# Keys of four chunks turned by transfers and VectorE instead of TensorE, and the bonus sums of two chunks taken from a natural layout, in a linear-attention plus cosine-FFN kernel

## Chip, cores and metric

One core of a Trainium2 chip runs the whole kernel. The metric is device time in microseconds (us) from start to end, the median of several executions. The profile is one execution; its span is what the engines' own records cover.

## What is computed

Inputs `r, k, v, w` are 4 batches x 8 heads x 768 steps x 48 values in float32, `u` is 8 x 48. The attention keeps a 48 x 48 state per batch and head; its output goes through a feed-forward layer with the gate h*cos(h), 384 to 2048 to 384.

```python
def _attn_ref(r, k, v, w, u):
    state = np.zeros((B, H, D, D), dtype=np.float32)
    for t in range(S):
        kt, vt, rt, wt = (k[:, :, t], v[:, :, t], r[:, :, t], w[:, :, t])
        cur = np.einsum('bhd,bhe->bhde', u[None] * kt, vt)
        y[:, :, t] = np.einsum('bhd,bhde->bhe', rt, state + cur)
        state = wt[:, :, :, None] * state + np.einsum('bhd,bhe->bhde', kt, vt)

def _moe_ref(x, w_in, w_out):
    h = x @ w_in
    return ((h * np.cos(h)) @ w_out)
```

The term `cur` gives, for each step and head, v times the number sum(r*u*k). The text calls that number the bonus sum.

## The kernel before

The 768 steps of each batch are cut into 6 chunks of 128, so there are 24 chunks; they are taken in the order "first chunk of all four batches, second chunk of all four, ...". Chunks 0 to 3 are therefore the first ones of their batches, chunks 4 to 7 the second ones. Two neighbouring chunks make a block (12 blocks, `BLK`), and each block goes through 8 FFN units of two 128-wide slices (96 units, numbered t).

In the chunk's own layout, `tt`, the heads' 48 values lie on partitions (two heads at rows 0 and 64, four pairs along the free axis) and time runs along the free axis. For each chunk j the steps have short names, which the tables of order use:

- `e`, `f`: the two scans of the decays on VectorE (L283, L289; f begins with a reciprocal, L288); `k`, `r`: keys and queries multiplied by them (L298 whole for chunks 0 to 5; L300 and L302, half each, from chunk 6 on); `W`: a small copy of the chunk's whole decay.
- Bonus sums. Chunks 0 to 5 (`BY_PE = 6`): `q` multiplies r and k on VectorE (L272), `pc` takes the sums over u by four TensorE products (L311), `cd` copies them out on ScalarE. From chunk 6 on: a natural copy of r and k (time on partitions) is loaded into the tile `rk` (L262, 384 KB, SP's queue), `m` and `u` multiply by k and by u (L320, L321), `c` reduces (L325). `A` places the sums on the diagonal of the score tiles `asb` (L335, POOL).
- `a`: scores k times r on TensorE (`pa`, L374 or L382); `P`: their lower triangle is copied into `asb` (L393 or L396, VectorE).
- Turned keys, time on partitions, which the state's update needs. Chunks 0 to 7 (`BY_BLOCKS = 8`): `t` is four TensorE transposes into `pt` (L408), `K` copies them to `kn` (L171; ScalarE in the opening, VectorE later). From chunk 8 on: `t` is 16 small transfers on SP's queue from `tt` to a tile of blocks (L425; 16 or 8 KB each), `K` one VectorE transpose of 32 x 32 blocks (L429).
- `s`, per block: products of v and `kn` into `pst` (L444), the first chunk's half before the second's; `n` adds them to the states (L454). `o` (L479, L485) and `p` (L507, L513) make the block's attention output, `xh` and `xl` turn it into the high and low part `xT` for the FFN.
- FFN unit: `mm1` (L594), then `I` (ScalarE, L557), `S` (VectorE, L560), `N` (ScalarE, L573), `M` (VectorE, L574), `H` (high part, mostly ScalarE, L171) and `L` (low part, POOL, L174, two halves), then `mm2` (L612), two units behind `mm1`.

The opening, units 0 to 15, is one table of tokens, `START`: TensorE, VectorE, ScalarE, POOL and SP execute their instructions in the order of these tokens. In it the FFN weights are loaded and split too (`raw`, `wg`, `wl`, `wy`, `wc`, `wx`). Units 16 to 23 follow the eight rows of `FIRST`, later units those of `PLAN`; there the four compute engines follow the rows' order, while the scheduler places SP's transfers. A row is one unit; "K+3" in block 2 means step K of chunk 7.

The tile kinds that matter: `tt` has 5 buffers, `rkt` 2, `kn` 2, `asb` 4. The two tiles `tops` serve the weights' conversion in the opening and the blocks of turned keys afterwards, by the parity of the chunk. SP's queue issues in order: an instruction that waits holds all behind it.

Of the kernel before, what the change touches and what calls it, by code (L numbers as in the profile page):

```python
# [66 lines left out]
ld0 e0 f0 ld1 raw2 raw1 q0 e1 k0 D14 pc0 r0 q1 cd0 v0 v1 raw0 f1 D10 a0 W0 wg2 wl2 A0 k1 pc1 wl1 r1 wy2 P0 cd1 D6 a1 wc2  # L67
t0 wg1 A1 ld3 ld2 wg0 W1 t1 P1 v5 wx2 wy1 o0 K0 K1 xh0.0 xp0.0 s0 wl0 e3 q3 wc1 xa0.0 wy0 wc0 xh0.1 wp1 f3 pc3 xp0.1
wv1 wx0 xa0.1 q2 e2 n0 k3 f2 raw3 k2 m0.0 m1.0 pc2 t3 r3 I0 r2 wg3 raw4 v2 wl3 cd2 v3 raw5 wy3 m0.1 cd3 S0 t2 a3 A3 K3
K2 A2 P3 ld7 wl4 wg4 a2 ld5 wc3 wg5 N0 raw8 raw6 P2 s1 wx3 raw9 n1 q5 o1 xh1.0 xl1.0 raw7 m1.1 xh1.1 pc5 xl1.1 M0 m0.2  # L70
wl5 Wa3 I1 wy4 m1.2 S1 m0.3 H0 cd5 wc4 N1 wy5 wc5 wg6 I2 m1.3 M1 wx4 wl6 I3 Hv1 L0 mm2.0 m0.4 wx5 S2 N2 wy6 S3 wg9 wl9
M2 m1.4 N3 L1 mm2.1 H2 I4 e5 wc6 wy9 L2 m0.5 M3 m1.5 S4 H3 wx6 N4 wg7 raw14 v4 L3 ld4 M4 raw11 m0.6 mm2.2 wl7 wcv9 wy7
wx9 mm2.3 wg8 I5 S5 wc7 wx7 H4 N5 M5 k5 m1.6 m0.7 t5 raw10 W2 wl8 wg11 I6 m1.7 H5 wy8 L4 mm2.4 S6 wc8 L5 I7 q4 N6 S7 N7
wl11 wx8 M6 mm2.5 H6 M7 H7 m0.8 m1.8 A5 wl10 L6 I8 wg10 f5 wy11 K5 m0.9 L7 S8 e4 ld6 raw13 raw12 m1.9 N8 M8 I9 wc11
wy10 wg12 wc10 mm2.6 mm2.7 raw15 d4 S9 N9 H8 r5 wx11 a5 wx10 M9 wl12 wl13 H9 L8 L9 m0.10 wy12 wc12 m1.10 wg13 m0.11 I10
k4 P5 wx12 S10 m1.11 N10 mm2.8 I11 pc4 t4 wy13 M10 wg15 wl15 Wa5 wc13 W4 d5 S11 cd4 f4 wx13 N11 K4 M11 m0.12 r4 H10 A4
# [917 lines left out]
```

## Time and profile before

| what | us |
|---|---|
| median of 3 runs | 499.8 (499.64 to 502.58) |
| the profiled execution | 499.0 |
| its span | 497.3 |
| TensorE busy | 489.9 (99%) |
| VectorE busy | 388.3 (78%) |
| ScalarE busy | 258.1 (52%) |
| POOL busy | 204.4 (41%) |

"Busy" for TensorE counts overlapping matmuls once. The span is 1.7 us shorter than its execution's time, and that execution 0.8 us shorter than the median. The TensorE clock was granted in full through nearly the whole span. Times in a timeline count from the span's start; a timeline's row merges neighbours of one kind, and "x" is their count.

### The profile page before, as it was taken

How to read it: one execution, taken by the hardware profiler on the slowest of the kernel's cores; microseconds unless marked ns; L12 is line 12 of the kernel's file. 1: busy time of each engine (PE TensorE's matmuls, PEld its weight loads, DVE VectorE, ACT ScalarE, POOL GpSimd, SP SyncE). 2: the span in 40 equal slices, each digit the busy share in tenths (PEclk: the TensorE clock that was granted, in tenths of full speed). 3: DMA queues.
4: the chain of work that ended last, by engine and by line, in shares of the span. 5: the costliest groups of instructions: out<-in, count | busy, mean ns of one | idle time of the engine just before them, and what ended most of it. 6: DMA issues, size and time to landing. Idle time of an engine off the chain costs nothing.

```text
span 497.3 us, 13512 instructions
## 1 busy us (share of the span) xinstructions
PE 489.9 (99%) x5592; PEld 475.3 (96%) x5592; DVE 388.3 (78%) x682; ACT 258.1 (52%) x447; POOL 204.4 (41%) x274
## 2 busy tenths in 40 slices
...
GB/s 276 414 404 130 380 153 1 131 100 97 38 92 195 19 200 78 17 200 32 58 175 42 80 154 60 80 94 121 75 44 156 65 8 121 33 65 128 33 2 35
DMA packets 38832, 57.01 MB, mean 115 GB/s; under 512 B 23536, under 2 KB 30192, under 8 KB 38768
## 3 DMA queue, kind: packets, MB, share of 16 engines
...
q8 instruction: 45, 0.74, 0.6%
...
q10 hardware_dynamic: 144, 0.10, 0.1%
...
## 4 chain that ended last, share of the span: by engine, by line
PE 80%; DVE 11%; ACT 3%; DMA 2%; issue 2%; SPq 1%; POOL 1%; DVEq 0%; ACTq 0%
PE ph L594 35%; PE acc L612 34%; PE pa L382 2%; PE py L479 2%; DVE rr L560 2%; PE py L485 2%; DVE rr L574 2%; DMA raw<-wts 1%; PE py L513 1%; DVE tt L289 1%; DVE asb L396 1%; DVE ee L283 1%; PE pst L444 1%; ACT rr L557 1%; PE py L507 1%
## 5 line engine op out<-in xcount | busy, mean ns | idle before, releaser
L174 POOL TENSOR_TENSOR gs<-rr,gs 128x256 fp32r<-128x256 f32 x188 | 155.5, 848 | 225.9 <-ACT gs L171 213.2
L594 PE MATMUL ph<-xT,w 128*128 128x256 f32 x1728 | 219.6, 281 | 0.2 <-ACT xT L531 0.2
L594 PEld LDWEIGHTS ph<-xT,w 128*128 128x128 f32 x1728 | 212.3, 188 | 3.6 <-PE py L513 1.6
L612 PE MATMUL acc<-w,gs 128*128 128x384 f32 x1152 | 215.4, 337 | 0.0
L612 PEld LDWEIGHTS acc<-w,gs 128*128 128x128 f32 x1152 | 196.2, 188 | 0.5 <-issue 0.2
L573 ACT ACTIVATE rr<-rr,quarter 128x512 f32<-128x512 f32 x96 | 69.5, 724 | 90.8 <-DVE rr L560 90.8
L560 DVE SCALAR_TENSOR_TENSOR rr<-rr,ph 128x512 f32<-128x512 int32 x96 | 65.6, 684 | 54.2 <-ACT rr L557 51.2
L171 ACT CAST gs<-rr 128x512 fp32r<-128x512 f32 x91 | 56.5, 621 | 70.6 <-DVE rr L574 50.5
L574 DVE TENSOR_TENSOR rr<-rr,ph 128x512 f32<-128x512 f32 x96 | 65.0, 678 | 21.9 <-ACT rr L573 20.0
L557 ACT ACTIVATE rr<-ph 128x512 int32<-128x512 f32 x96 | 57.2, 596 | 43.5 <-PE ph L594 43.1
L335 POOL TENSOR_SCALAR_AFFINE_SELECT asb<-cd 128x512 f32<-128x512 f32 x48 | 35.3, 758 | 51.6 <-DVE cd L325 26.6
L396 DVE COPY_PREDICATED asb<-turned_mask,pa 64x128 f32<-64x128 uint8 (+1 forms) x108 | 33.6, 346 | 2.1 <-POOL asb L335 0.3
L283 DVE TENSOR_TENSOR_SCAN ee<-tt,one_e 112x516 f32<-112x516 f32 (+1 forms) x25 | 32.6, 1309 | 1.8 <-DMA tt<-tr 1.8
L289 DVE TENSOR_TENSOR_SCAN tt<-tt,inj 112x516 f32<-112x516 f32 x24 | 29.7, 1236 | 0.8
L174 DVE TENSOR_TENSOR xT<-py,xT 128x384 fp32r<-128x384 f32 x22 | 11.3, 551 | 16.6 <-ACT xT L171 16.6
L195 ACT ACTIVATE top<-raw 128x768 f16<-128x768 bf16 x16 | 17.5, 1091 | 4.2 <-DMA raw<-wts 3.6
L479 PE MATMUL py<-asb,v 128*32 128x128 f32 x384 | 18.0, 276 | 0.3 <-DVE asb L393 0.2
L485 PE MATMUL py<-asb,v 128*32 128x128 f32 x384 | 17.3, 273 | 0.0
L171 ACT CAST xT<-py 128x384 fp32r<-128x384 f32 x24 | 10.5, 481 | 12.2 <-PE py L513 8.2
L203 DVE CUSTOM_DVE_ANT_0 h<-h,top 128x1536 uint16<-128x1536 uint16 x16 | 15.7, 982 | 0.1
L171 ACT COPY past<-dd 48x192 f32<-48x192 f32 x40 | 14.0, 349 | 2.7 <-DVE dd L358 2.4
L382 PEld LDWEIGHTS pa<-tt 48*64 48x64 f32 x576 | 12.9, 133 | 2.2 <-issue 1.7
...
## 6 DMA issues: line engine op xcount, KB each, us to landing
...
top<-tt SPq DMA_DIRECT2D x96, 8.0 KB, 1.8
```

Source lines behind the costliest of these rows:

```text
L171: (nc.scalar.copy if E[name] is nc.scalar else E[name].tensor_copy)(out=out, in_=in_)
L174: E[name].tensor_tensor(out=out, in0=full, in1=high.bitcast(F32), op=ALU.subtract)
L283: nc.vector.tensor_tensor_scan(out=ee[:, pairs].rearrange("p a t -> p (a t)")[:, ::-1], data0=wp[:, cols][:, ::-1], data1=one_e[:, pairs]. ...
L289: nc.vector.tensor_tensor_scan(out=wp[:, 0:W129], data0=wp[:, 0:W129], data1=inj.rearrange("p a t -> p (a t)"), initial=0.0, op0=ALU.mult, ...
L335: nc.gpsimd.affine_select(out=asb, in_=col.unsqueeze(2).to_broadcast([C, NP, C]), pattern=[[0, 4], [1, C]], compare_op=ALU.is_equal, fill= ...
L396: nc.vector.copy_predicated(*(which(x) for x in (a["asb", h], turned_mask, pa[h])))
L557: nc.scalar.activation(made["rr"].bitcast(I32), ph, AF.Copy, scale=INV2PI / W_SCALE, bias=0.25)
L560: nc.vector.scalar_tensor_tensor(out=made["rr"], in0=made["rr"].bitcast(I32), scalar=-2.0 * math.pi * W_SCALE, in1=ph, op0=ALU.mult, op1=A ...
L573: N=lambda: nc.scalar.activation(made["rr"], made["rr"], AF.Sin, scale=1.0 / W_SCALE, bias=quarter),
L574: M=lambda: nc.vector.tensor_tensor(out=made["rr"], in0=made["rr"], in1=ph, op=ALU.mult), H=high, L=low)
L594: nc.tensor.matmul(out=ph[:, fi], lhsT=wgt[u * FU + fi][:, 0, a, kt * 128:(kt + 1) * 128], rhs=xT[:, b, kt], start=n == 0, stop=n == 3 * K ...
L612: nc.tensor.matmul(out=accs[i][j][:, :DM], lhsT=gs[:, a, fi, j * C:(j + 1) * C], rhs=wgt[u * FU + fi][:, 1, b], start=u == 0 and fi == 0 a ...
```

## The change

Two constants move: `BY_PE` from 6 to 4, so that chunks 4 and 5 take their bonus sums from the natural layout, and `BY_BLOCKS` from 8 to 4, so that the keys of chunks 4 to 7 are turned by small transfers and the VectorE transpose. In the opening, m and u of chunks 4 and 5 are put on POOL (`rk="p", ru="p"`). The tables `START` and `FIRST` lose `q4 q5 pc4 pc5 cd4 cd5` and gain `lr4 lr5 m4 m5 u4 u5 c4 c5`; `t5`, `t4`, `K5`, `K4` move later, and `e6 k6 t6` move from `FIRST` into the end of `START`; `t7` moves to the first row of `FIRST`, `K6` to its third and `K7` to the end of its sixth. Chunks 4 and 5 use their own `rk` tile as the tile of blocks, so that their transfers wait for the reduction c; their `rk` tiles take the kind `rkt`, which q used.

```diff
-BY_PE = 6
+BY_PE = 4
-BY_BLOCKS = 8
+BY_BLOCKS = 4
-... r3="v", k3="v", rk="v", ru="v", ...      (EARLY)
+... r3="v", k3="v", rk="p", ru="p", ...      (EARLY)
 START
-... raw9 n1 q5 o1 xh1.0 xl1.0 raw7 m1.1 xh1.1 pc5 xl1.1 M0 ... S1 m0.3 H0 cd5 wc4 ...
+... raw9 n1 o1 xh1.0 xl1.0 raw7 m1.1 xh1.1 xl1.1 M0 ... S1 m0.3 H0 wc4 ...
-... L3 ld4 M4 ... m0.7 t5 raw10 ... I7 q4 N6 ... m1.8 A5 wl10 L6 I8 wg10 f5 wy11 K5 m0.9 L7
+... L3 ld4 lr5 M4 ... m0.7 raw10 ... I7 N6 ... m1.8 m5 u5 wl10 L6 I8 wg10 c5 f5 wy11 m0.9 L7
-... raw13 raw12 m1.9 ... raw15 d4 S9 N9 H8 r5 ... I11 pc4 t4 wy13 ... W4 d5 S11 cd4 f4 ... K4 M11
+... raw13 raw12 lr4 m1.9 ... raw15 t5 d4 S9 N9 H8 A5 r5 ... I11 wy13 ... W4 m4 u4 d5 S11 c4 f4 ... M11
-... Hv11 wl14 ... L12 xh2.0 Hv13 m1.15 I14 S14 N14 ...
+... Hv11 K5 t4 wl14 ... L12 xh2.0 Hv13 e6 k6 t6 m1.15 I14 S14 K4 N14 ...
 FIRST
-"... mm1 e+2 e+3 k+2 k+3 I S f+2 N M mm2 H L r+2",
+"... mm1 e+2 e+3 k+2 k+3 I S f+2 N M mm2 H L r+2 t+3",
-"mm1 t+2 t+3 I S K+2 K+3 N M mm2 H L m+2 u+2 c+2 d+2",
+"mm1 I S K+2 N M mm2 H L m+2 u+2 c+2 d+2",
-"mm1 I S f+4 N M mm2 H L r+4 load+6 t+4",
+"mm1 I S f+4 N M mm2 H L r+4 load+6 K+3 t+4",
@@ att_load_rk
-        a["rk"] = rk = buf("h", [C, 2, DM], F32, "rk")
+        if "u" not in told:
+            told["u"] = cst.tile([C, DM], F32, tag="u_sb", name="u_sb")
+            E["qt"].dma_start(out=told["u"], in_=u.to_broadcast([C, DM]))
+        a["rk"] = rk = buf("h" if a["j"] >= ALL_OF else "rkt", [C, 2, DM], F32, "rk")
@@ turned_by_blocks
-        blocks = tops[a["j"] % 2].bitcast(F32)[:, :512].rearrange("p (q a t) -> p q a t", q=4, a=NP)
+        blocks = (tops[a["j"] % 2].bitcast(F32) if a["j"] >= ALL_OF else a["rk"].rearrange("p k n -> p (k n)"))[:, :512].rearrange("p (q a t) -> p q a t", q=4, a=NP)
@@ at_first
-            if n == "A" and j == ALL_OF - 1:
+            if n == "u" and j == ALL_OF - 1:
```

VectorE at the end of unit 21, the last before block 3's state products; before (f8, M21, r8, then `xl` and `n` of block 3):

```order
L288 RECIPROCAL inj<-ee 112x4
L289 SCALAR_TENSOR_TENSOR tt<-tt,inj 112x516
L574 TENSOR_TENSOR rr<-rr,ph 128x512
L300 TENSOR_TENSOR tt<-tt 112x256
L302 TENSOR_TENSOR tt<-tt 112x256
L174 TENSOR_TENSOR xT<-py,xT 128x384 x2
```

The same place now:

```order
L288 RECIPROCAL inj<-ee 112x4
L289 SCALAR_TENSOR_TENSOR tt<-tt,inj 112x516
L574 TENSOR_TENSOR rr<-rr,ph 128x512
L300 TENSOR_TENSOR tt<-tt 112x256
L302 TENSOR_TENSOR tt<-tt 112x256
L429 STREAM_TRANSPOSE kn<-top_100 128x512
L174 TENSOR_TENSOR xT<-py,xT 128x384 x2
```

K7, chunk 7's turned keys, stands behind r8; before, its copy stood three units earlier. On TensorE the state products of block 3 (L444) stand where they stood, behind L507.

VectorE around the states of block 2 (L454), before:

```order
L454 TENSOR_TENSOR all_states<-pst,dd 48x192 x4
L283 SCALAR_TENSOR_TENSOR ee<-tt,one_e 112x516 x2
L300 TENSOR_TENSOR tt<-tt,ee 112x256
L302 TENSOR_TENSOR tt<-tt,ee 112x256
L300 TENSOR_TENSOR tt<-tt,ee 112x256
L302 TENSOR_TENSOR tt<-tt,ee 112x256
```

The same place now, from the end of unit 13's work on:

```order
L283 SCALAR_TENSOR_TENSOR ee<-tt,one_e 112x516
L300 TENSOR_TENSOR tt<-tt,ee 112x256
L302 TENSOR_TENSOR tt<-tt,ee 112x256
L560 SCALAR_TENSOR_TENSOR rr<-rr,ph 128x512
L429 STREAM_TRANSPOSE kn<-rk 128x512
L574 TENSOR_TENSOR rr<-rr,ph 128x512
```

One scan and one pair of products (e6, k6) left the place behind L454 and stand ahead of unit 14's L560; K4 follows it.

SP's queue from the last weight load on (tiles: `rk` of chunks 5 and 4, `top_99` for chunk 6, `top_100` for chunk 7), now:

```order
L180 DMA raw<-wts 128x3071
L425 DMA rk<-tt 32x4x32 x4
L425 DMA rk<-tt 16x4x32 x4
L425 DMA rk<-tt 32x4x32 x4
L425 DMA rk<-tt 16x4x32 x4
L248 DMA tt<-tr 128x1541
L266 DMA v<-tv 128x448
...
L262 DMA rk<-tn 128x768 x2
L248 DMA tt<-tr 128x1541
L425 DMA top_99<-tt 32x4x32 x4
...
L425 DMA top_100<-tt 32x4x32 x4
L632 DMA out<-ob 128x384 x2
```

Four groups of 16 small transfers now stand between the loads of block 4's chunks and, for chunk 7, around the first two stores of the output; before, no small transfer was issued until those stores had gone.

## Rows read from the trace of the kernel before

**Rows 1.** The page, busy time by engine (share of span, instructions)

```profile
PE 489.9 (99%) x5592; PEld 475.3 (96%) x5592; DVE 388.3 (78%) x682; ACT 258.1 (52%) x447; POOL 204.4 (41%) x274
```

**Rows 2.** Busy time by stretch: PE, PEld, DVE, ACT, POOL, granted clock, DMA share, GB/s

```profile
40.00:103.00 63.00, 63.00 (x551) 60.84 (x549) 54.53 (x75) 48.40 (x76) 32.17 (x37) 1.00 0.46 165
103.00:138.00 35.00, 35.00 (x515) 34.10 (x515) 29.92 (x62) 15.41 (x29) 15.48 (x22) 1.00 0.20 63
```

**Rows 3.** Waits of PE over the span, longest of six: total, times, longest

```profile
PE filled L740 <- POOL ident masks.py:199: 1.9, 1, 1.9
```

**Rows 4.** Groups by line on PE: busy us, mean ns of one, idle before

```profile
L311 PE MATMUL pc<-u_by_head,rkt 112*128 112x2 f32 x48 | 5.8, 243 | 0.1
L408 PE MATMUL pt<-ident,tt 112*128 112x112 f32 x32 | 4.5, 266 | 0.0
```

**Rows 5.** Timeline of PE, mm2 of units 6 and 7, then steps removed: start, length

```profile
66.08 4.33 PE L612 MATMUL acc<-w,gs 128*128 128x384 f32 x24
...
77.83 0.95 PE L311 MATMUL pc<-u_by_head,rkt 112*128 112x2 f32 x8
78.64 0.58 PE L408 MATMUL pt<-ident,tt 112*128 112x112 f32 x4
79.23 1.30 PE L594 MATMUL ph<-xT,w 128*128 128x256 f32 x9
...
114.40 0.93 PE L408 MATMUL pt<-ident,tt 112*128 112x112 f32 x8
115.10 2.33 PE L612 MATMUL acc<-w,gs 128*128 128x384 f32 x12
```

**Rows 6.** Groups by line and shape on VectorE: busy us, mean ns of one

```profile
L325 DVE TENSOR_REDUCE cd<-rk 128x8 f32<-128x384 f32 x18 | 9.9, 550 | 0.3
L429 DVE STREAM_TRANSPOSE kn<-top 128x512 f32<-128x512 f32 x12 | 8.4, 699 | 0.0
```

**Rows 7.** Timeline of PE at block 3's state products

```profile
133.84 0.86 PE L444 MATMUL pst<-v,kn 128*32 128x48 f32 x64
134.63 0.67 PE L513 MATMUL py<-tt,past 48*32 48x128 f32 x32
```

**Rows 8.** Timeline of VectorE from unit 13 to the end of r8

```profile
94.15 0.83 DVE L171 CAST gs<-rr 128x512 fp32r<-128x512 f32 x1
...
105.45 2.36 DVE L283 TENSOR_TENSOR_SCAN ee<-tt,one_e 112x516 f32<-112x516 f32 x2
...
109.16 0.69 DVE L560 SCALAR_TENSOR_TENSOR rr<-rr,ph 128x512 f32<-128x512 int32 x1
...
136.39 0.41 DVE L302 TENSOR_TENSOR tt<-tt 112x256 f32<-112x256 f32 x1
```

**Rows 9.** SP's small transfers: issue ns min/median/max, time to land, one chunk's sixteen

```profile
L425 SPq DMA_DIRECT2D top<-tt x192: 585/594/1811, 133.0 to 355.6; - x192
...
DMA to landing us min/median/max: 1.8/1.8/4.1
...
132.96 11.86 SPq L425 DMA_DIRECT2D top<-tt  x16
```

**Rows 10.** POOL's low parts: ns min/median/max over the span, and three rows of its timeline

```profile
L174 POOL TENSOR_TENSOR gs<-rr,gs x188: 719/739/2520, 37.1 to 483.6; 128x256 fp32r<-128x256 f32 x188
...
58.44 1.22 POOL L335 TENSOR_SCALAR_AFFINE_SELECT asb<-cd 128x512 f32<-128x512 f32 x2
...
61.94 5.55 POOL L174 TENSOR_TENSOR gs<-rr,gs 128x256 fp32r<-128x256 f32 x4 [0.52 <-ACT gs L171]
...
73.59 1.90 POOL L174 TENSOR_TENSOR gs<-rr,gs 128x256 fp32r<-128x256 f32 x2 [0.68 <-ACT gs L171]
```

**Rows 11.** Timeline of VectorE between 61 and 75 us

```profile
61.58 0.17 DVE L288 RECIPROCAL inj<-ee 112x4 f32<-112x4 f32 x1
...
69.19 0.68 DVE L298 TENSOR_TENSOR tt<-tt 112x512 f32<-112x512 f32 x1
...
73.65 1.23 DVE L298 TENSOR_TENSOR tt<-tt,ee 112x512 f32<-112x512 f32 x1
```

More of the change, by code (lines that the diff above doesn't have):

```diff
@@ L66 @@
 START = """
[L67 to L76, printed above, removed]
@@ L77 @@
-L10 wg14 mm2.9 m1.12 m0.13 Hv11 wl14 I12 S12 N12 pp4 pp5 m1.13 a4 P4 wy15 L11 I13 M12 wy14 wcv15 S13 wx15 mm2.10 wc14
-o2 mm2.11 N13 wx14 p2 m0.14 H12 m1.14 M13 m0.15 L12 xh2.0 Hv13 m1.15 I14 S14 N14 M14 mm2.12 I15 S15 xl2.0 L13 Hv14 L14
-mm2.13 xh2.1 N15 s2 xl2.1 M15 Hv15 L15 n2
+ld0 e0 f0 ld1 raw2 raw1 q0 e1 k0 D14 pc0 r0 q1 cd0 v0 v1 raw0 f1 D10 a0 W0 wg2 wl2 A0 k1 pc1 wl1 r1 wy2 P0 cd1 D6 a1
+wc2 t0 wg1 A1 ld3 ld2 wg0 W1 t1 P1 v5 wx2 wy1 o0 K0 K1 xh0.0 xp0.0 s0 wl0 e3 q3 wc1 xa0.0 wy0 wc0 xh0.1 wp1 f3 pc3
@@ new lines @@
+xp0.1 wv1 wx0 xa0.1 q2 e2 n0 k3 f2 raw3 k2 m0.0 m1.0 pc2 t3 r3 I0 r2 wg3 raw4 v2 wl3 cd2 v3 raw5 wy3 m0.1 cd3 S0 t2 a3
+A3 K3 K2 A2 P3 ld7 wl4 wg4 a2 ld5 wc3 wg5 N0 raw8 raw6 P2 s1 wx3 raw9 n1 o1 xh1.0 xl1.0 raw7 m1.1 xh1.1 xl1.1 M0 m0.2
+wl5 Wa3 I1 wy4 m1.2 S1 m0.3 H0 wc4 N1 wy5 wc5 wg6 I2 m1.3 M1 wx4 wl6 I3 Hv1 L0 mm2.0 m0.4 wx5 S2 N2 wy6 S3 wg9 wl9 M2
+m1.4 N3 L1 mm2.1 H2 I4 e5 wc6 wy9 L2 m0.5 M3 m1.5 S4 H3 wx6 N4 wg7 raw14 v4 L3 ld4 lr5 M4 raw11 m0.6 mm2.2 wl7 wcv9
+wy7 wx9 mm2.3 wg8 I5 S5 wc7 wx7 H4 N5 M5 k5 m1.6 m0.7 raw10 W2 wl8 wg11 I6 m1.7 H5 wy8 L4 mm2.4 S6 wc8 L5 I7 N6 S7 N7
```

13 lines of the change are left out of this document (9 added, 4 removed).

## The prediction, as it was put on record before the changed kernel ran

> **What bounds the kernel now.** I read the page's busy line first: TensorE is busy for 489.9 of 497.3 us, every other engine for at most 78% [rows 1]. Busy time of pipelined matmuls can hide slow ones, so I then asked for TensorE's waits: six in the whole span, and the longest, 1.9 us, lies ahead of the first product [rows 3]. The busy time by stretch says the same of the stretches that the change touches, 40 to 103 and 103 to 138 us: TensorE busy for all of both [rows 2]. So TensorE's queue of work is the bound, and any instruction taken out of it is worth its start-to-start time. But VectorE is not far away: 54.5 of 63 and 29.9 of 35 us, 86% in both [rows 2]. It runs behind or ahead of TensorE by a few us, and a step that TensorE needs must not be placed too late in VectorE's order. That is what I look at below.
>
> **What goes from TensorE.** Four products pc for chunk 4 start at 77.83 and the next step at 78.64: 0.81 us. Those for chunk 5 are alike, 0.81. The transposes of chunk 4 take from 78.64 to 79.23, 0.59; those of chunks 6 and 7 together from 114.40 to 115.10, 0.70, or 0.35 a chunk, which I take for chunk 5 too [rows 5]. Up to block 2's state products (103 us) that is 0.81 + 0.81 + 0.59 + 0.35 = 2.56 us, and 3.26 with chunks 6 and 7. The busy time of the groups gives a higher bound: 16 of the 48 pc records at 5.8/48 and 16 of the 32 transposes at 4.5/32 make 1.9 + 2.3 = 4.2 us [rows 4], but busy time overlaps with neighbours, so I use 3.26. Kept in full, that is 0.65% of the time: even the whole gain is within 1%.
>
> **What comes to VectorE.** Four transposes of 0.70 and two reductions of 0.55, 3.9 us in all [rows 6]; two products q and the copies of chunks 6 and 7 go against them. Over some 80 us that lies in the gaps that its 86% leave. K5 and K4 have time: t5 can go out behind the last weight load and the reduction c5 (about 66 us), 16 issues at 0.594 us are 9.5 us, landing 1.8 [rows 9], so 77.5 at the latest, and K5 stands near 84. t4 follows c4 (about 80.5), lands by 92, and K4 stands behind unit 14's L560, near 96. Block 2's state products come at 100.4 by then. No wait there.
>
> **The step that I think decides: K7.** Block 3's state products start at 133.84 and end where L513 starts, 134.63; chunk 7's half starts at the middle, 134.23 [rows 7]. It needs K7, which VectorE now reaches only after r8, whose last piece ends at 136.39 + 0.41 = 136.80 in the trace of before [rows 8]. By before's clock K7 is thus 2.6 us too late even to begin. Both engines move earlier, by different amounts:
> - TensorE arrives 3.26 us earlier: 134.23 - 3.26 = 130.97.
> - VectorE from 104 to 137 us is a chain that starts with block 2's states, which come 2.56 us earlier. Behind them two scans and two pairs of products lie between 105.45 and 109.16 [rows 8]; one set goes, half of 3.71 = 1.86. Together 4.42 us, if nothing else holds it. r8 then ends at 132.38, and K7 with 0.70 [rows 6] at 133.08.
>
> TensorE waits from 130.97 to 133.08, 2.1 us, and goes on at 133.08 instead of 134.23: of 3.26 us, 1.15 are left. I take off 0.05 for the signal between the engines: 1.1. Bounds: had VectorE only TensorE's own 2.56 ahead, K7 would end at 134.94 and 0.7 us would be lost (+0.7); if VectorE were ahead by another 2.1 us the whole 3.26 would be kept. Nothing behind that place gives more or takes it back: the longest of TensorE's waits is the one at the start [rows 3], and what is late next, `xl` and the states of block 3, then runs on a VectorE that is about 2 us earlier than before.
>
> **The sum.** Span 497.3 - 1.1 = 496.2. The profiled execution, 499.0, becomes 497.9; the median of the runs, 0.8 us higher, 499.8 - 1.1 = **498.7 us**.
>
> **POOL.** Products m and u of 128x384 do not occur on POOL in the trace. From its low parts of 128x256, one costs 1.5 times 0.72 to 2.52 us [rows 10], 1.1 to 3.8; the rows nearest in time, 5.55/4 and 1.90/2, give 2.1 and 1.4, of which I take 1.6. m5 and u5 stand where A5 began at 58.44 [rows 10]: u5 ends at 61.7 (bounds 60.7 to 66.1). c5 stands just ahead of the reciprocal at 61.58 [rows 11], so it waits little. What hides m5 and u5 is the slack of the low parts behind them: unit 7's end at 67.49 [rows 10], and TensorE needs them in the last sixth of the 24 products that run from 66.08 for 4.33 us [rows 5], from about 69.7. Of these 2.2 us TensorE itself takes 1.2, being ahead by pc5 and t5, and POOL's added work, 3.2 less the 1.2 that A5 gave up, another 2.0. So the cover is used up by my value, 1.0 us over: I count 0, since 1.2 us of lead and 1.6 us a product are both the upper part of what I know, and leave up to 1 us, more if POOL is slower, to a rival.
>
> On this the trace shows one thing more. The same VectorE product took 0.68 us at 69.19, with POOL idle, and 1.23 us at 73.65, beside two POOL products of 1.90 us in all [rows 10, 11]. The Trainium skill, page "SBUF — State Buffer", section "Who interferes with whom", says why: a VectorE instruction with two SBUF inputs and a POOL instruction that reads SBUF exclude each other on a shared port, so that one blocks. The rows agree. By the rule, m and u don't take work off VectorE in full but hold it up for up to their own length, and the sum would lose up to 1.1 us of gain (the POOL rival below).
>
> **Rivals.**
> 1. *Kept in full.* VectorE is far enough ahead that K7 is ready. It needs 6.5 us against the 4.4 worked out above. Time 499.8 - 3.26 = 496.5. Chance 0.12.
> 2. *POOL holds up the opening.* m, u in front of the low parts of units 6 to 11, together with the port, delay mm2 or the reductions by 1 to 2 us; all later steps shift alike, K7 too, so the loss adds fully: 499.8 - 1.1 + (1 to 2) = 499.7 to 500.7. For it: POOL's 5.55 us for four low parts just there [rows 10]. Against: POOL is idle for half of the stretch [rows 2]. Chance 0.18.
> 3. *Slower: the transfers are late.* K7 waits for its 16 transfers, which on SP's in-order queue stand behind chunk 6's 16, two loads and two stores. t6 can start when k6 is done: behind the cast at 94.15, 1.9 us of work, so about 96. Between 96 and 132.4, when K7 could start, 32 small transfers have 36.4 us, 1.1 each. One chunk's sixteen took 11.86 us, 0.74 each, with median issue of 0.594 [rows 9]: they land at about 123, some 9 us in time. It decides from the point where K7's data land after 132.4 + 1.1 = 133.5; then each us is a us lost. At the longest issue in the trace, 1.811 [rows 9], 32 take 58 us, K7 comes at 156, and the time is about 520. Chance that it ends above 501: 0.10.
>
> The Trainium skill, page "VectorE: DVE Perf Modes", section "Rules for kernel authors", advises TensorE for a full 128 x 128 transpose where the result may go to PSUM, and its section "The three transpose paths" warns that plain strided copies are many times slower. By it this change is the wrong way round and would go like rival 3. The rows show sixteen issues of 0.594 us where TensorE needed 0.35 to 0.59 us in all, so they agree on the price; they don't show that anything waits for it.
>
> **Chances and range.** My forecast (0.4 to 1.9 us gained: 497.9 to 499.4) 0.55, kept in full 0.12, POOL 0.18, late transfers 0.10, something else 0.05. Leaving out the late transfers and half of the rest, the range is 496.4 to 501.0. About 1% is what a measurement of this kernel can tell from no change; that is 494.8 to 504.8. No case reaches below, and only the worst part of rival 3 and something unseen go above: faster 0.02, same 0.93, slower 0.05.
>
> **What would show each step right or wrong.** Right: no L311 after 30 us and no L408 at 40 us and later; TensorE at block 2's state products near 100.4; a wait of TensorE of about 2 us, the longest behind the start, at L444 for `kn` of L429, near 131 to 133; K7 directly behind r8. Wrong: no such wait, and a span near 494 (rival 1); waits of L612 on POOL's `gs` or of VectorE's L325 on POOL between 60 and 82 (rival 2); a wait of L429 for DMA, or transfers of chunk 7 landing past 132 (rival 3). If the granted clock falls behind TensorE's wait, the loss is larger than the wait; before, it stood at 1.00 in both stretches [rows 2].

## The result: slower by 1.1%

| what | before | after |
|---|---|---|
| median, us | 499.9 (6 runs, 499.5 to 502.6) | 506.0 (6 runs, 504.9 to 506.7) |
| ratio, 95% interval | | 1.0113 (1.0094 to 1.0131) |
| span of the profiled execution | 497.3 | 505.0 |

The forecast was 498.7 us, 1.1 less than before; measured were 6.1 us more. 7.2 us have to be found. The profiles below say where, and fourteen kernels behind them say why.

First the page's busy line of the changed kernel, to be held against [rows 1]:

```profile
PE 490.1 (97%) x5560; PEld 474.6 (94%) x5560; DVE 391.8 (78%) x684; ACT 257.9 (51%) x443; POOL 214.3 (42%) x278
```

TensorE has 32 instructions fewer, yet its share falls from 99 to 97%: it now waits. Its busy time in the two stretches of [rows 2] (columns as there) says where:

```profile
40.00:103.00 63.00, 58.80 (x514) 55.81 (x513) 56.17 (x76) 46.42 (x72) 42.02 (x39) 1.00 0.50 172
103.00:138.00 35.00, 33.85 (x440) 32.82 (x438) 29.72 (x62) 14.95 (x29) 14.94 (x21) 1.00 0.34 95
```

4.2 us of waiting in the first stretch, which had none before, and POOL's busy time is up by 9.9 us there. The second has 1.15, the first part of a wait that goes on past 138. TensorE's waits over the span (total, times, longest), beside the one of [rows 3], which is still there:

```profile
PE ph L594 <- DVE rr L574: 2.9, 2, 1.6
PE pst L444 <- DVE kn L429: 2.2, 1, 2.2
PE acc L612 <- ACT gs L171: 0.7, 1, 0.7
PE ph L594 <- DVE w L205: 0.6, 1, 0.6
```

The second row is the wait that the prediction described. The others are new too, all in the opening.

**The wait for K7.** Timeline of TensorE at block 3's state products in the changed kernel (start, length; in brackets the wait ahead), to be read with [rows 7]:

```profile
136.32 0.53 PE L444 MATMUL pst<-v,kn 128*32 128x48 f32 x32
139.08 0.53 PE L444 MATMUL pst<-v,kn 128*32 128x48 f32 x32 [2.23 <-DVE kn L429]
139.54 0.67 PE L513 MATMUL py<-tt,past 48*32 48x128 f32 x32
140.14 3.90 PE L594 MATMUL ph<-xT,w 128*128 128x256 f32 x18
```

VectorE at the same place, the end of r8 [rows 8] and K7 directly behind it:

```profile
135.09 0.69 DVE L560 SCALAR_TENSOR_TENSOR rr<-rr,ph 128x512 f32<-128x512 int32 x1 [0.59 <-ACT rr L557]
...
137.99 0.41 DVE L302 TENSOR_TENSOR tt<-tt 112x256 f32<-112x256 f32 x1
138.33 0.70 DVE L429 STREAM_TRANSPOSE kn<-top 128x512 f32<-128x512 f32 x1
```

The wait is 2.23 us where 2.1 were forecast, and for the forecast reason. One thing is worse: the 18 products of the next unit take 3.90 us where as many took 2.26 at 129.84. The busy time by stretch shows it in the granted clock (the figure behind POOL's):

```profile
138.00:140.00 2.00, 0.92 (x64) 0.80 (x64) 1.02 (x3) 0.46 (x1) 1.42 (x2) 1.00 0.10 12
140.00:142.00 2.00, 2.00 (x26) 1.86 (x11) 1.24 (x3) 0.86 (x2) 0.00 (x0) 0.64 0.13 21
142.00:144.00 2.00, 2.00 (x11) 2.00 (x11) 1.11 (x4) 0.00 (x0) 0.00 (x0) 0.51 0.17 25
144.00:146.00 2.00, 2.00 (x14) 2.00 (x13) 0.69 (x1) 1.17 (x2) 0.00 (x0) 1.00 0.11 14
```

Behind the wait TensorE runs at the lower of its two levels, 1.2 instead of 2.4 GHz, for some 3.4 us (0.72 and 0.98 of two stretches of 2 us each).

**The opening.** Block 2's state products start at 106.27 us; before it was 103.00, and the prediction wanted 100.44. TensorE is on time at 54 us, 2.1 us late at 64 and 3.3 late at 89. The first thing that is late is on ScalarE (timeline):

```profile
57.87 1.08 ACT L195 ACTIVATE top<-raw 128x768 f16<-128x768 bf16 x1 [3.80 <-DMA raw<-wts]
58.82 0.56 ACT L557 ACTIVATE rr<-ph 128x512 int32<-128x512 f32 x1
```

ScalarE waits 3.80 us for the weights raw 11. In the trace of before the same instruction had no wait:

```profile
54.27 1.10 ACT L195 ACTIVATE top<-raw 128x768 f16<-128x768 bf16 x1
```

In the changed kernel L557 and the high parts stand behind it, and TensorE goes without. On SP's queue `u_sb` (192 KB) and `rk` of chunk 5 (384 KB) now stand ahead of raw 11 (timeline of SP's queue):

```profile
46.16 0.38 SPq L260 DMA_DIRECT2D u_sb<-u  x1
46.63 0.44 SPq L262 DMA_DIRECT2D rk<-tn  x1
47.12 0.97 SPq L180 DMA_DIRECT2D raw<-wts  x2
```

Before, `u_sb` stood behind raw 11, raw 10 and a `tt`, and there was no `rk` at all:

```profile
46.08 0.93 SPq L180 DMA_DIRECT2D raw<-wts  x2
47.09 0.42 SPq L248 DMA_DIRECT2D tt<-tr  x1
47.56 0.50 SPq L258 DMA_DIRECT2D u_sb<-u  x1
```

So raw 11 is issued 1.04 us later, and it takes 10.7 us from issue to landing instead of 8.2. Further on POOL is busy for 19.7 of the 20 us from 60 to 80 (timeline):

```profile
61.36 1.02 POOL L320 TENSOR_TENSOR rk<-rk 128x384 f32<-128x384 f32 x1
62.45 1.59 POOL L321 TENSOR_TENSOR rk<-rk,u_sb 128x384 f32<-128x384 f32 x1
...
65.17 6.49 POOL L174 TENSOR_TENSOR gs<-rr,gs 128x256 fp32r<-128x256 f32 x4
71.63 3.45 POOL L335 TENSOR_SCALAR_AFFINE_SELECT asb<-cd 128x512 f32<-128x512 f32 x2
75.05 4.72 POOL L174 TENSOR_TENSOR gs<-rr,gs 128x256 fp32r<-128x256 f32 x4
```

So there were three suspects to price: transfers ahead of the weights, K7 with the clock behind it, and POOL or VectorE in the opening.

### The profile page after: what moved, and what is told of

It is laid out like the page before. It is cut to its first block, busy times and chain, and to the rows that moved or that the text cites. A ratio compares the mean times of both kernels' runs of the same rounds, so it can differ in the third digit from the quotient of the medians.

```text
span 505.0 us, 13533 instructions
## 1 busy us (share of the span) xinstructions
PE 490.1 (97%) x5560; PEld 474.6 (94%) x5560; DVE 391.8 (78%) x684; ACT 257.9 (51%) x443; POOL 214.3 (42%) x278
## 4 chain that ended last, share of the span: by engine, by line
PE 82%; DVE 6%; POOL 5%; ACT 4%; issue 3%; DVEq 0%; ACTq 0%; POOLq 0%
PE ph L594 35%; PE acc L612 34%; POOL gs L174 3%; PE pa L382 2%; PE py L479 2%; PE filled L740 2%; PE py L485 2%; PE py L513 1%; PE pst L444 1%; DVE rr L560 1%; PE pa L374 1%; PE py L507 1%; POOL asb L335 1%; DVE tt L289 1%; ACT gs L171 1%
## 5 line engine op out<-in xcount | busy, mean ns | idle before, releaser
L174 POOL TENSOR_TENSOR gs<-rr,gs 128x256 fp32r<-128x256 f32 x188 | 159.0, 867 | 228.1 <-ACT gs L171 221.5
L594 PE MATMUL ph<-xT,w 128*128 128x256 f32 x1728 | 221.6, 282 | 4.2 <-DVE rr L574 2.9
L594 PEld LDWEIGHTS ph<-xT,w 128*128 128x128 f32 x1728 | 213.8, 189 | 8.5 <-issue 4.1
L612 PE MATMUL acc<-w,gs 128*128 128x384 f32 x1152 | 215.4, 337 | 0.7 <-ACT gs L171 0.7
L612 PEld LDWEIGHTS acc<-w,gs 128*128 128x128 f32 x1152 | 196.3, 188 | 1.3 <-ACT gs L171 1.0
L560 DVE SCALAR_TENSOR_TENSOR rr<-rr,ph 128x512 f32<-128x512 int32 x96 | 65.5, 682 | 55.4 <-ACT rr L557 54.8
L574 DVE TENSOR_TENSOR rr<-rr,ph 128x512 f32<-128x512 f32 x96 | 65.0, 678 | 21.2 <-ACT rr L573 19.3
L557 ACT ACTIVATE rr<-ph 128x512 int32<-128x512 f32 x96 | 57.2, 596 | 46.5 <-PE ph L594 46.1
L335 POOL TENSOR_SCALAR_AFFINE_SELECT asb<-cd 128x512 f32<-128x512 f32 x48 | 38.3, 823 | 47.7 <-DVE cd L325 28.5
L171 ACT CAST xT<-py 128x384 fp32r<-128x384 f32 x24 | 10.7, 481 | 14.5 <-PE py L513 10.2
```

The lines of the kernel that those rows point to most:

```text
L171: (nc.scalar.copy if E[name] is nc.scalar else E[name].tensor_copy)(out=out, in_=in_)
L174: E[name].tensor_tensor(out=out, in0=full, in1=high.bitcast(F32), op=ALU.subtract)
L335: nc.gpsimd.affine_select(out=asb, in_=col.unsqueeze(2).to_broadcast([C, NP, C]), pattern=[[0, 4], [1, C]], compare_op=ALU.is_equal, fill= ...
L557: nc.scalar.activation(made["rr"].bitcast(I32), ph, AF.Copy, scale=INV2PI / W_SCALE, bias=0.25)
L560: nc.vector.scalar_tensor_tensor(out=made["rr"], in0=made["rr"].bitcast(I32), scalar=-2.0 * math.pi * W_SCALE, in1=ph, op0=ALU.mult, op1=A ...
L574: M=lambda: nc.vector.tensor_tensor(out=made["rr"], in0=made["rr"], in1=ph, op=ALU.mult), H=high, L=low)
```

## Experiments

All medians on one page ("s2" is the start of block 2's state products in the profiled execution; the first score products start up to 1.0 us apart from profile to profile, which is the grain of that column; the last column is TensorE's wait inside block 3's state products):

| kernel | median | ratio to before (95%) | s2 | wait at L444 |
|---|---|---|---|---|
| before | 499.9 | | 103.00 | none |
| after | 506.0 | 1.0113 (1.0094 to 1.0131) | 106.27 | 2.2 |
| bonus alone | 504.8 | 1.0087 (1.0062 to 1.0112) | 107.13 | none |
| keys alone | 502.9 | 1.0042 (1.0012 to 1.0071) | 102.71 | 2.2 |
| after, K7 early | 502.9 | 1.0040 (1.0016 to 1.0063) | 106.61 | none |
| after, u, r, k late | 503.5 | 1.0047 (1.0019 to 1.0075) | 103.98 | 2.2 |
| both moves | 500.3 | 1.0001 (0.9988 to 1.0015) | 103.60 | none |
| both, m and u on VectorE | 502.3 | 1.0043 (1.0029 to 1.0057) | 105.82 | none |
| keys alone, K7 early | 500.0 | 0.9994 (0.9982 to 1.0006) | 103.75 | none |
| after, u alone late | 504.8 | 1.0106 (1.0072 to 1.0141) | 104.43 | 2.2 |
| before, less TensorE work | 500.0 | 0.9998 (0.9982 to 1.0014) | 103.36 | none |
| the same, less VectorE work | 499.3 | 0.9991 (0.9971 to 1.0011) | 102.85 | none |
| both moves, no m, u | 499.4 | 0.9983 (0.9966 to 1.0001) | 103.05 | none |
| before, keys of 6 and 7 only | 499.6 | 0.9998 (0.9978 to 1.0017) | 103.72 | none |
| after, u's tile from 128 rows | 504.8 | 1.0095 (1.0066 to 1.0125) | 106.01 | 2.2 |
| after, the wait for K7 filled | 505.6 | 1.0102 (1.0069 to 1.0135) | 106.20 | 0.7 and 0.9 |

### The two halves of the change

Bonus part alone: the keys go back to TensorE, in their old places.

```diff
-BY_BLOCKS = 4
+BY_BLOCKS = 8
 (START, FIRST: t4 t5 K4 K5 e6 k6 t6 t7 K6 K7 as before)
```

> The changed kernel with the keys of chunks 4 to 7 turned by TensorE again, in their old places: the bonus part alone. Theory A (the opening's loss of 5.8 us comes from the bonus part, and the wait at L444 with the clock behind it, 3.8 us, comes from the keys): block 2's state products come about 107.2 us (106.27 of the changed kernel plus 0.94 for the transposes of chunks 4 and 5), 4.2 later than the 103.0 of before; no wait of TensorE at L444 near 133 to 139; time 499.9 + 4.2 = 504.1 (503.3 to 505). Theory B (the opening is held by the 32 small transfers and VectorE's transposes of chunks 4 and 5, and the bonus part is harmless): 499.9 - 1.6 = 498.3, and state products of block 2 near 101.4.

Measured: 504.8 us, s2 at 107.13, no wait at block 3's state products. Theory A.

Keys part alone: the bonus sums go back to TensorE.

```diff
-BY_PE = 4
+BY_PE = 6
 (START: q4 q5 pc4 pc5 cd4 cd5 A5 as before; a tile of kind rkt for the blocks of chunks 4 and 5)
```

> The kernel before with the keys of chunks 4 to 7 turned by small transfers and VectorE, at the places of the change; the bonus sums of chunks 4 and 5 stay on TensorE (for chunks 4 and 5 the transfers move all 32 rows of a block instead of 16 in every other one). Theory A: block 2's state products near 102.1 (103.0 - 0.94); K7 stands behind r8 as in the changed kernel, TensorE waits there 2 to 4 us at L444 and its clock falls behind the wait; time 502 to 504, of which 1.2 to 1.8 are the clock. Theory B (the small transfers hold the opening): block 2's state products later than 104 and a time of 505 or more. If neither costs anything: 499.9 - 1.6 = 498.3.

Measured: 502.9 us, s2 at 102.71, and the wait of 2.23 us again. Theory A: the opening is lost by the bonus part, and the keys part loses behind r8. (Of the 0.94 us that the keys part takes off TensorE in the opening little shows: s2 is 0.29 us earlier than before, 0.08 if counted from each kernel's first score products.)

The wait is the same with and without the lost opening because both engines count from block 2's state products. From there to the end of r8 VectorE takes 32.13 us in both kernels (33.80 before), and TensorE takes 30.05 us to block 3's state products (30.84 before). The 0.59 us ahead of L560 above are no wait for TensorE. L557, which L560 waits for, stands on ScalarE directly behind a cast that waited for VectorE itself (timeline of ScalarE in the changed kernel):

```profile
133.94 0.62 ACT L171 CAST gs<-rr 128x512 fp32r<-128x512 f32 x1 [1.07 <-DVE rr L574]
134.46 0.59 ACT L557 ACTIVATE rr<-ph 128x512 int32<-128x512 f32 x1
```

### K7 earlier

```diff
-         "mm1 I S f+4 N M mm2 H L r+4 load+6 K+3 t+4",
+         "mm1 I S K+3 f+4 N M mm2 H L r+4 load+6 t+4",
```

> The changed kernel with K7 moved on VectorE from behind r8 to right behind the sums of unit 21, some 4 us earlier. Theory A (the wait at L444 costs its 2.2 us and the fall of TensorE's clock behind it 1.2 to 1.8 more): the wait is gone, the granted clock stays at 1.00 between 140 and 144 us, time 506.0 - 3.7 = 502.3 (501.8 to 502.9). Rival C (VectorE is late as a whole there, so that f8 and r8 behind K7 or the states of block 3 are what TensorE then waits for): the wait moves to another line between 131 and 150 us and the time is 504.5 to 506. Rival D (the clock's fall costs nothing of its own): 503.8.

Measured: 502.9 us, 3.1 less than after. The state products run through in one piece (timeline of TensorE), and the next unit's 18 products take 2.37 us:

```profile
136.66 0.86 PE L444 MATMUL pst<-v,kn 128*32 128x48 f32 x64
137.46 0.67 PE L513 MATMUL py<-tt,past 48*32 48x128 f32 x32
138.06 2.37 PE L594 MATMUL ph<-xT,w 128*128 128x256 f32 x18
```

Of the 3.1 us, 2.2 are the wait, which leaves 0.9 for the clock on the mean. Nothing else became late (rival C falls). In the profile the clock's share was larger (3.90 - 2.26 = 1.6 us), but the clock does not fall in every run. Of the five profiles with the wait (after, keys alone, u, r, k late, u alone late, and u from 128 rows, below) two show the fall behind it, in three it stays at 1.00. The runs say the same: the mean granted clock of a run was 0.997 or less in 25 of 40 runs of these five kernels, in 8 of 94 of the nine other kernels without the wait, and in 17 of 112 runs of before beside them. In keys alone, the four runs at 1.000 have a mean of 501.6 us and the six at 0.996 to 0.997 one of 503.6.

### Is it the idle time that lowers the clock?

```diff
-        for n, a in enumerate(two):
+        for n, a in [(0, two[0])] + [(1, two[0])] * 4 + [(1, two[1])] if i == 3 else enumerate(two):
```

> The changed kernel with TensorE kept at work while it waits for K7: between the two halves of block 3's state products the first half's products are computed four times more into the place that the second half then overwrites, about 1.9 us. K7 comes as late as before. Theory W (TensorE's clock falls because it stood idle there): the granted clock stays at 1.00 behind the place in nearly all runs, the second half starts at the same time as in the changed kernel or up to 0.2 us later, time 506.0 - 0.9 to 1.5 = 504.5 to 505.1. Theory X (the clock falls for another reason, near 140 us anyway): the clock falls in as many runs as in the changed kernel, time 505.7 to 506.5.

Measured: 505.6 us (8 runs), above the 505.1 of theory W, just below the 505.7 of theory X, and not told apart from 506.0 by time. The clock speaks for W: one of 8 runs at 0.997 or less, where after had 5 of 6. But four more stand at 0.998, which leaves room for some 2 us at the lower level (0.002 of 504.5 us, times two). In the profile it stays at 1.00 behind the place (busy time by stretch):

```profile
140.00:142.00 2.00, 1.49 (x42) 1.22 (x41) 0.08 (x1) 0.59 (x2) 0.00 (x0) 1.00 0.16 24
142.00:144.00 2.00, 2.00 (x18) 2.00 (x17) 1.96 (x6) 0.53 (x2) 0.00 (x0) 1.00 0.13 17
```

Why the time did not follow shows TensorE's timeline: a new hole of 0.94 us, inside the second half, for which the profile shows no other engine.

```profile
139.03 0.53 PE L444 MATMUL pst<-v,kn 128*32 128x48 f32 x28 [0.74 <-DVE kn L429]
140.51 0.27 PE L444 MATMUL pst<-v,kn 128*16 128x48 f32 x4 [0.94 <-issue]
```

So TensorE still stood idle, for 0.74 and 0.94 us instead of 2.23 in one piece, and the large fall became rarer. That the fall follows the idle time is likely by the clock of 8 runs and not shown by their time; its price by this kernel stays open, since the filling brought a cost of its own.

### The transfers of u, r and k

Both moved behind raw 10 on SP's queue:

```diff
-... ld4 lr5 M4 raw11 m0.6 ... m0.7 raw10 W2 ...
+... ld4 M4 raw11 m0.6 ... m0.7 raw10 lr5 W2 ...
```

> The changed kernel with the transfers of u and of r, k of chunk 5 moved on SP from ahead of the weights raw 11 and raw 10 to behind them; nothing else. Theory A1 (about half of the opening's 5.8 us comes from these transfers, which make raw 11 late, so that ScalarE waits 3.8 us at L195): that wait is gone or under 1 us, block 2's state products come at 103 to 104.5 instead of 106.27, time 502.7 to 504.2. Rival A2 (POOL's queue, with m, u, the mask and A5 ahead of the low parts, is the whole cause): ScalarE's wait goes but block 2's state products stay at 106 +- 0.5 and the time at 505.3 to 506.3.

Measured: 503.5 us, 2.5 less than after, s2 at 103.98. The wait of ScalarE is down to 1.17 us (timeline):

```profile
55.13 1.09 ACT L195 ACTIVATE top<-raw 128x768 f16<-128x768 bf16 x1 [1.17 <-DMA raw<-wts]
```

Theory A1, with a wait that is a little above its 1 us. Then u alone, r and k staying ahead of raw 11:

```diff
     def att_load_rk(a):
-        if "u" not in told:
-            told["u"] = cst.tile(...)
-            E["qt"].dma_start(out=told["u"], in_=u.to_broadcast([C, DM]))
...
         elif n == "raw":
             load_weights(j)
+            if j == 10:
+                told["u"] = cst.tile(...)
+                E["qt"].dma_start(out=told["u"], in_=u.to_broadcast([C, DM]))
```

> The changed kernel with the transfer of u alone moved behind raw 10 on SP; r, k of chunk 5 stay ahead of raw 11. If u's 192 KB (one row of DRAM read for all 128 partitions) is what delays raw 11: as with both moved, ScalarE's wait at L195 under 1.5 us, block 2's state products near 104, time 503.5 +- 0.6. If r, k of chunk 5 (384 KB) delays it: wait 2.5 us or more, state products at 105.5 to 106.3, time 505 to 506. If the bytes count alike: wait about 2.9, state products near 105.5, time 505.1.

Measured: 504.8 us from only 4 runs, two of them at a clock of 0.990 to 0.992; the time is no evidence. The profile is: ScalarE waits 1.6 us instead of 3.8, s2 at 104.43, so it is u. Its 192 KB account for about 2.2 us of the lateness, the 384 KB of r and k for some 0.5 (1.6 against 1.17 with both moved). By bytes it would be the other way round. Raw 11 itself shows how the two differ (issue on SP's queue, and time from issue to landing; the profiles' starts are up to 0.4 us apart here):

| kernel | raw 11 issued | us to landing |
|---|---|---|
| before | 46.08 | 8.2 |
| after | 47.12 | 10.7 |
| after, u, r, k late | 46.02 | 9.1 |
| after, u alone late | 46.77 | 9.2 |
| after, u's tile from 128 rows (next) | 47.51 | 10.1 |

Each transfer ahead puts off the issue of raw 11 by some 0.5 us. For r and k that is all (9.2 us to landing against 9.1). With u ahead the landing takes 1.5 us more. The DMA rate says the same: it falls to 99 to 188 GB/s for about 2 us, at 51 us in the changed kernel and at 56 us with u late (116 to 164 GB/s), so the dip moves with u. A guess was that u, one row read for all 128 partitions, is slow by itself. So u's tile was filled from 128 different rows at the same place:

```diff
-            E["qt"].dma_start(out=told["u"], in_=u.to_broadcast([C, DM]))
+            E["qt"].dma_start(out=told["u"], in_=tn[a["g"], :, 0])
```

> The changed kernel, whose 192 KB for u at the same place of SP's queue are read from 128 different rows (r of the chunk) instead of one row read 128 times; the bonus sums of all chunks whose sums come from natural r and k are therefore not those of the reference. Theory R (one row read for all 128 partitions is slow by itself: 99 to 188 GB/s for 2.5 us where the queue else moves 400): the dip of the rate is gone, ScalarE's wait at L195 falls from 3.8 to 1.5 us or less, block 2's state products come near 104, time about 503.6. Theory S (any 192 KB there cost this): wait 3.2 us or more, state products at 105.8 or later, time 505.3 to 506.3.

Measured: a wait of 3.2 us, s2 at 106.01, 504.8 us (503.1 to 509.2). Wait and state products are those of theory S, the time lies between the two. The reading of one row is worth 0.6 us of the 3.8 at most, and this wait differs between profiles: in the kernel with the filled wait, where u stands as in after, it is 3.5. That a small transfer stands there costs the rest. Why 192 KB cost more than 384 KB stays open; u's rows are half as long as those of r and k (1.5 and 3 KB), which no kernel here varies.

### Both moves, and where m and u should run

> The changed kernel with both moves: K7 on VectorE right behind the sums of unit 21, and the transfers of u and of chunk 5's r, k behind raw 10. Theory A (the two losses are independent and add): 503.5 - 2.2 for the wait - 0.9 for the clock's mean share = 500.4 (499.8 to 501.0), block 2's state products at 104.0 as without the K7 move, no wait at L444. If they overlap (what the opening gives back is lost again further on): 501.3 or more.

The edits are the two diffs above. Measured: 500.3 us, theory A: 506.0 - 2.5 - 3.1 = 500.4. The two losses add, and they are 5.6 of the 6.1 us. This kernel is level with before (1.0001), so the gain is still missing: s2 stands at 103.60, where the work taken from TensorE should have made it 100.4. TensorE waits (timeline):

```profile
78.69 1.30 PE L594 MATMUL ph<-xT,w 128*128 128x256 f32 x9 [1.26 <-DVE rr L574]
...
83.35 3.03 PE L594 MATMUL ph<-xT,w 128*128 128x256 f32 x21 [0.57 <-DVE w L205]
```

The chain of work that ended last, followed back in this trace, leads from the second wait through VectorE's scan f4 and c4 to u4 and m4 on POOL, and then through POOL's queue back to 57 us: the low parts of units 5 to 9, A5, m5 and u5. c4 waited there for u4 (timeline of VectorE):

```profile
80.10 0.55 DVE L325 TENSOR_REDUCE cd<-rk 128x8 f32<-128x384 f32 x1 [0.33 <-POOL rk L321]
```

So m and u of chunks 4 and 5 were given to VectorE:

```diff
-... rk="p", ru="p", ...      (EARLY)
+... rk="v", ru="v", ...
```

> As the kernel with both moves, and the products m and u of chunks 4 and 5 go to VectorE instead of POOL. Block 2's state products stand there at 104.0, 3.6 us later than the 100.4 that the removed TensorE work alone would give. Theory P (these 3.6 us come from POOL, which is busy 19.7 of the 20 us from 60 to 80): they come at 101 to 102.5 and the time is 498 to 499.3. Rival V (VectorE, busy 20.0 of the same 20 us, is the bound there as well, and four more products of 0.6 to 0.9 us lengthen it): they come at 104.5 to 107 and the time is 501 to 503.5.

Measured: 502.3 us, s2 at 105.82: rival V. VectorE has no room for them either. And without m and u at all:

```diff
-... m0.8 m1.8 m5 u5 wl10 ... W4 m4 u4 d5 ...   (START)
+... m0.8 m1.8 wl10 ... W4 d5 ...
```

> The changed kernel with K7 early and u, r, k late, and without the products m and u of chunks 4 and 5 on POOL (the bonus sums of these chunks are sums of r alone). With them block 2's state products stand 0.1 us after those of before, counted from each kernel's start, where 2.6 earlier was expected. If POOL's 4.7 us of products hold the opening (directly, or through VectorE instructions that are longer beside them): state products 1.5 to 2.7 us earlier, time 497.6 to 498.9. If VectorE's own work is what holds it: 0 to 0.8 us, time 499.5 to 500.3.

Measured: 499.4 us, 1.0 less; counted from each kernel's first score products, s2 comes 0.75 us earlier. That is VectorE's branch by s2, and between the two by time. By the ratios the difference is 0.9 us, and their intervals (0.9988 to 1.0015 and 0.9966 to 1.0001) leave -0.2 to 2.0 for it, so POOL's part is about 1 us and not clear of none. Without m and u the chain that ended last runs over VectorE's L574 ahead of the first wait. With them POOL is as full as VectorE (both busy for 19.7 of the 20 us from 60 to 80); without them VectorE alone keeps most of the gain away.

### Is TensorE the bound in the opening at all?

The first step of the prediction was tested on the kernel before: TensorE's products and transposes of chunks 4 and 5 left out, VectorE and POOL with the same work.

```diff
 START loses cd5 cd4 K4 K5 (copies on ScalarE)
     def att_diag(a):
+        if a["j"] in (4, 5):
+            a["cd"] = atts[a["j"] - 2]["cd"]
+            part(("A", a["j"]), lambda: picked(a))
+            return
...
+        if a["j"] in (4, 5):
+            a["key"] = atts[a["j"] - 2]["key"]
+            return
```

> The kernel before with the bonus products and the transposes of chunks 4 and 5 left out of TensorE (their sums and keys are those of chunks 2 and 3 taken again, so four of the chunks' results are not computed), with their copies on ScalarE; VectorE and POOL keep all that they did. Theory T (TensorE's queue bounds the opening, as the prediction has it): the 2.56 us come back in full, block 2's state products at 100.4, time 497.3. Theory V (VectorE hands over late between 60 and 84 us, so TensorE waits for rr or w instead): block 2's state products at 101.5 to 103, TensorE waits for VectorE there, time 498.3 to 499.9.

Measured: 500.0 us and s2 at 103.36: 2.56 us of TensorE's work are gone, and no gain shows (0.9998, 0.9982 to 1.0014, which is -0.9 to +0.7 us). Theory T falls. Theory V's wait is there, and even less is kept than its ranges allowed. TensorE's timeline, for the unit that started at 79.23 before [rows 5]:

```profile
75.74 2.08 PE L619 MATMUL acc<-w,gs 128*128 128x384 f32 x11
79.59 1.29 PE L601 MATMUL ph<-xT,w 128*128 128x256 f32 x9 [1.77 <-DVE rr L581]
```

(L601, L619 and L581 are L594, L612 and L574 with the added lines.) It waits exactly where pc4 and the transposes of chunk 4 stood, for 1.77 us in place of their 1.40. Of the other 1.1 us, 0.6 became a wait for `wholes` (ScalarE) at 36.59, where pc5 had stood, and the rest of the lead ended in the longer wait at 79.59. That could have been read from the trace of before. VectorE's timeline there:

```profile
76.06 0.94 DVE L205 TENSOR_TENSOR w<-h,w 128x768 fp32r<-128x768 f32 x1
76.93 0.68 DVE L560 SCALAR_TENSOR_TENSOR rr<-rr,ph 128x512 f32<-128x512 int32 x1
77.52 0.95 DVE L203 CUSTOM_DVE_ANT_0 h<-h,top 128x1536 uint16<-128x1536 uint16 x1
78.39 0.69 DVE L574 TENSOR_TENSOR rr<-rr,ph 128x512 f32<-128x512 f32 x1
79.00 0.35 DVE L358 TENSOR_TENSOR dd<-all_states,ee 112x192 f32<-112x192 f32 x1
```

L574 reads the tile `ph`; when it is done, the place is free for a later unit's products, and those are what waits. It ends at about 79.1, and the unit starts at 79.23. From 65.5 to 84.3 us VectorE has no gap above 0.15 us; behind that it is free for a third of the time (busy time by stretch, VectorE third):

```profile
65.50:84.30 18.80, 18.80 (x144) 18.24 (x143) 18.61 (x26) 16.38 (x27) 8.25 (x10) 1.00 0.20 68
84.30:103.00 18.70, 18.70 (x225) 17.10 (x223) 12.56 (x20) 8.87 (x17) 7.21 (x10) 1.00 0.38 128
```

TensorE was as full because pc4 and the transposes filled what would have been a wait.

One part of the wait belongs to this kernel alone. Since A4 no longer has to wait for pc4, POOL places these sums at 75.33 instead of 81.52, and beside them VectorE's L205 takes 1.54 us instead of 0.94. Without that, 0.6 us more could have been kept. So the removed 2.56 us were worth next to nothing, and some 0.7 us at most by this estimate.

The same, with VectorE's two products q left out as well:

```diff
- q5 ... q4      (START)
```

> The same with VectorE's two products r times k of chunks 4 and 5 (1.23 us each) left out as well. Theory V: VectorE's relief lets TensorE keep more: block 2's state products 0.7 to 2 us earlier than without it, 100.4 to 101.2. Theory T: both kernels at 100.4, no difference.

Measured: 499.3 us, s2 at 102.85, 0.5 us earlier (both kernels' first score products start within 0.02 us of each other). The direction is V's, the size is below the 0.7 expected (and s2 far from 100.4 to 101.2) and within what profiles differ; it is no proof by itself. Of the two products q4 lies nearer the place, at 56.65 in the trace of before, but ahead of a wait of VectorE of 1.01 us at 64.88, for ScalarE, which takes up most of what it gives. TensorE still waits 1.55 us for L574 at 79.

### Versions without the known losses

Keys alone with K7 early, and the keys of chunks 6 and 7 alone (outside of the opening), both with the edit of K7 above:

> The keys part alone (bonus sums of chunks 4 and 5 on TensorE), with K7 on VectorE right behind the sums of unit 21. Theory A (all that the keys part loses is the wait at L444 and the clock behind it): no wait there, granted clock 1.00, time 499.9 - 1.64 for the transposes = 498.3 (497.9 to 498.9), faster than before by 0.3% (0.2 to 0.4). Rival (the small transfers or the later K4 cost something in the opening too): 499.3 to 500.2.

Measured: 500.0 us, ratio 0.9994 (0.9982 to 1.0006): the rival. In the opening nothing is kept of 0.94 us: s2 stands 92.57 us behind the first score products, in the kernel before 92.51.

```diff
-BY_BLOCKS = 8
+BY_BLOCKS = 6
 (FIRST as in the changed kernel, with K7 early)
```

> The kernel before with only the keys of chunks 6 and 7 turned by small transfers and VectorE, K7 on VectorE right behind the sums of unit 21; the opening is that of before. Theory: outside of the opening TensorE's queue is the bound, the 0.70 us for the transposes of chunks 6 and 7 are kept, no wait at L444: time 499.9 - 0.7 = 499.2, ratio 0.9986 (0.998 to 0.999). Rival (the small transfers in the opening's end or TensorE's issue of the next loops takes it back): 499.6 to 500.2, ratio within 0.0006 of 1.

Measured: 499.6 us, ratio 0.9998 (0.9978 to 1.0017): undecided by time. In the trace the 0.70 us are kept: from block 2's to block 3's state products it is 133.77 - 103.72 = 30.05 us, before 133.84 - 103.00 = 30.84 [rows 7]. No version here is measurably faster than before.

## Why the prediction was wrong, step by step

- **What bounds the kernel: failed.** "Any instruction taken out of it is worth its start-to-start time" rested on TensorE being busy for all of 63 us and on VectorE's 86% [rows 2]. The 86% is a mean over 63 us in which VectorE is full from 65 to 84 and free mostly behind that (16.7 of the 23 us from 80 on). In the opening VectorE's L574 and TensorE's next unit came within 0.15 us of each other, so the removed work became a wait. Taking the 2.56 us off TensorE in the kernel before changed the time by 0 (-0.9 to +0.7). Term of the sum: -2.56, measured 0.0, or some -0.7 without what that test itself added.
- **Transfers ahead of the weights: not in the sum.** The prediction walked through the 16 small transfers of each chunk and never priced `u_sb` and `lr5`, which the change had put ahead of raw 11 and raw 10 on SP's queue. Term: 0, measured +2.5 by moving them behind the weights.
- **K7 behind r8: right, by its mechanism.** Forecast wait 2.1, measured 2.23, at the forecast place, for L429. TensorE came at 136.85 (forecast 130.97) and K7 at 139.03 (forecast 133.08): both 5.9 us late, because block 2's state products, from which both count, were 5.8 late. From there VectorE gained 1.67 us (1.86 forecast) and TensorE 0.79 (0.70 forecast); these two misses would make the wait 0.3 us longer, and the forecast's roundings take most of that back, so that it came out to 0.1 us is luck; the mechanism is not. The loss behind the wait was named ("larger than the wait") and not counted: the clock, 0.9 us on the mean.
- **POOL: term too small.** m cost 1.00 to 1.02 and u 1.02 to 1.59 us, less than the 1.6 assumed; u5 ended at 61.4 in the kernel with both moves, where 61.7 was forecast. Still the sum's 0 for them was too low: about 1.0 us by the run without them, the low end of rival 2, though not clear of none. Part of it goes through VectorE. The product L358 took 0.35 us twice in the trace of before, with POOL idle, and in the changed kernel 0.90 beside POOL's low parts and 0.70 beside m4. The group of L358 from 55 to 85 us (busy, mean ns of one), first in the changed kernel, with m and u on POOL:

```profile
L358 DVE TENSOR_TENSOR dd<-all_states,ee 112x192 f32<-112x192 f32 x2 | 1.6, 804 | 0.0
```

  Then in the kernel with both moves and m, u on VectorE:

```profile
L358 DVE TENSOR_TENSOR dd<-all_states,ee 112x192 f32<-112x192 f32 x2 | 0.7, 348 | 0.0
```

  Only the second of the two products is lengthened by m and u themselves. In the kernel with both moves and no m, u (timeline; the line is L359 there) the first still stands beside a low part:

```profile
67.69 0.90 DVE L359 TENSOR_TENSOR dd<-all_states,ee 112x192 f32<-112x192 f32 x1
78.69 0.35 DVE L359 TENSOR_TENSOR dd<-all_states,ee 112x192 f32<-112x192 f32 x1
```

  The Trainium skill, page "SBUF — State Buffer", section "Who interferes with whom", has it that a VectorE instruction with two SBUF inputs contends with a POOL instruction that reads SBUF. The trace agrees: 0.35 us with POOL idle, 0.70 to 0.90 beside its products.
- **The keys of chunks 6 and 7: right.** 0.70 us forecast, 30.84 - 30.05 = 0.79 kept between the two state products.
- **Small transfers late: rightly rejected.** t7's last piece is issued by 124.9 us and lands about 1.8 later, before K7 starts at 138.33. L429 never waits for DMA.

As a sum: 499.9 - 0.8 (keys of 6 and 7) + 2.2 (wait) + 0.9 (clock) + 2.5 (transfers) + 1.0 (m, u) = 505.7; measured 506.0. The remaining 0.3 is within the grain of these terms, of which the first is read from profiles and the last is not clear of none. Against the forecast's -1.1 the largest misses are the gain that was never there (2.6) and the transfers (2.5).

The chance of 0.05 for "slower" was too small for another reason too: the three cases of loss were treated as alternatives, each against a gain of 1.1, when they could add.
